# Gated linear attention and a token/channel mixer on one core: decays by small DMAs, the last batch's transposes by DMA, and a fixed instruction list

## The chip, the cores and the metric

The kernel runs on one core of a Trainium2 chip. The metric is device time in microseconds (us) of one execution, the median of three runs. The engines are TensorE (PE), VectorE (DVE), ScalarE (ACT), GpSimd (POOL) and SyncE (SP); each works through its own instructions in order and waits on semaphores for the others. Here POOL issues the input loads, SP issues stores and some loads.

## The reference

Inputs q, k, v and f_logit have 4 batches, 8 heads, 768 tokens and 48 features per head. Then follows a mixer over tokens and channels with four weight matrices.

```python
f = 1.0 / (1.0 + np.exp(-f_logit))
for t in range(S):
    state = f[:, :, t, :, None] * state + np.einsum('bhd,bhe->bhde', k[:, :, t], v[:, :, t])
    y[:, :, t] = np.einsum('bhd,bhde->bhe', q[:, :, t], state)
...
h = np.maximum(xt @ w_tok1, 0.0) @ w_tok2          # over tokens
u = x + h.transpose(0, 2, 1)
h2 = np.maximum(u @ w_ch1, 0.0) @ w_ch2            # over channels, 384 -> 1536 -> 384
out = u + h2
```

Here x is y with its 8 heads laid side by side, 768 x 384 per batch.

## The kernel before, in words

The 768 tokens of a batch b are cut into 6 chunks c of 128. Line numbers are those of the kernel before.

- *Gates* (L448): ACT makes L = ln(1 + exp(-f_logit)) with two passes (L455, L456). L is kept in fp32; its upper 16 bits are read as a bf16 number, and DVE or POOL puts the remainder into Llo (L461). Batch 0's chunks 3 to 5 use the fp32 form instead.
- *Sums* (L514): a matmul with a triangular matrix gives the running sum over the chunk's tokens (L528 and L529, or L517 in fp32). Beside it, for all chunks but the last, single-column matmuls with a vector of ones give the total over the chunk for each feature (L526, L527, or L519 in fp32), already laid out with features on partitions.
- ACT makes G = exp(-sum), Gi = exp(sum) (L539, L541) and from the totals glast = exp(-total), the decay of the state over the chunk (L544, 128 x 4).
- DVE makes q x G and k x Gi (L549). PE transposes both with an identity matrix, 8 transposes of 128 x 128 per chunk (L559); DVE or ACT copies the result from PSUM to qkT (L566, L572).
- *Scores* (L478): 8 matmuls of qkT with itself; DVE multiplies them by the triangle into AmT (L596). *Parts* (L494): k^T v for the state.
- *State* (L605, L608, L610 on DVE): state = (state + part) x glast. Two copies spread it into a block-diagonal bf16 tile (L615).
- *y* (L627, L634): qkT times the spread state, plus AmT times v; copied to x_bf and x_nat.
- *Mixer* per batch (L659): tok1 (L664), relu to h1T, tok2 (L680), sums into x_nat and u_bf, transposes of u_bf (L715) into uT, then ch1 (L732, 72 matmuls of 384 columns), relu to zT (L444 on ACT, L446 on DVE), ch2 (L751, 75 matmuls), the sum on DVE (L757) and the store by SP (L761).

The order of all work comes from a planner in the kernel (`Plan`, L104): each operation has a rank, costs per engine and a set of operations before it, and a table SHIFTS replaces rank and lag of some. The planner repeatedly takes the operation and engine with the earliest start plus lag, then the lowest rank, and emits the operations in the order of their planned starts. Where it sees PE idle in the first 25.5 us, it fills in dummy matmuls (L798). Work of neighbouring batches is interleaved: the attention of batch b + 1 runs between the ch1 and ch2 matmuls of batch b.

Loads: SP loads f of batch 0 chunk by chunk, held back by marks that POOL sets (L363); POOL loads k, q, v of batch 0 by chunk, the weights, and the later batches, those of batch 3 whole (L377, L384). The DMA on POOL's queue also casts fp32 to bf16. The triangle and the identity are made on POOL by a library (masks.py).

Of the kernel before, what the change touches and what calls it, by code (L numbers as in the profile page):

```python
# [16 lines left out]
WAKE = {PE: 55, ACT: 38, DVE: 38, POOL: 66, SP: 30}  # L17
NBANK = 8
RING = 16384
SHIFTS = (  # L20
# [57 lines left out]
)  # L78
KEPT = 3
SPLIT = 3  # L80


class Op:
    def __init__(self, engines, rank, fn, need, make, bank, kind):
        self.engines, self.rank, self.fn, self.kind = engines, rank, fn, kind
        self.need, self.make, self.bank = need, make, bank
        self.before: set = set()
        self.behind = None
        self.after: list = []
        self.missing = 0  # L90
        self.start = self.end = None
        self.engine = None
        self.tail = None
        self.room = 1
        self.lag = 0.0


class Bank:
    def __init__(self):
        self.users = 0  # L100
        self.at = None


class Plan:  # L104

    def __init__(self):  # L110
        self.ops = []
        self.maker: dict = {}
        self.users: dict = {}
        self.loads = {POOL: [], SP: []}

    def add(self, engines, rank, fn, need=(), make=(), bank=None, kind=("fix", 100, 100), tail_of=None, room=1):


        engines = (engines,) if isinstance(engines, str) else engines
        op = Op(engines, rank, fn, need, make, bank, kind)  # L120
        for key in need:
# [710 lines left out]
```

## Time and profile before

| | |
|---|---|
| Median of 3 runs | 182.77 us (182.35 to 183.07) |
| Span of the profiled execution, first to last instruction | 180.3 us |
| What lies around the span, from the median | 2.5 us |
| PE busy, matmuls | 171.1 us, 1811 |
| DVE, ACT, POOL busy | 129.6, 109.4, 86.2 us |
| First ch1 matmul (L732) starts | 34.20 us |
| Packets of POOL's DMA queue, share of 16 engines' span | 97.7% |

The record gives no other time of the profiled execution than its span, so the 2.5 us is the median less that span. Busy time of PE is the union of its matmuls' durations, and these overlap: a 384-column matmul is listed with 326 ns. The chain that ended last follows the work back from the last instruction; its rows give start, length and what it was. A releaser behind an arrow is what ended a wait.

### The profile page before, as it was taken

The page shows a single profiled execution, that of the slowest core. Times are in us where ns is not written, and L with a number is a line of the kernel's source. Part 1 is how long each engine was busy: PE and PEld are TensorE (multiplying, and loading weights), DVE is VectorE, ACT ScalarE, POOL GpSimd, SP SyncE. Part 2 cuts the span into 40 slices and gives each one's busy share as a digit, 9 for nine tenths or more (in the row PEclk, how much of TensorE's full clock was granted, in tenths as well). Part 3 has the DMA queues.
Part 4 walks back from the last instruction along what each step waited for, and adds up shares of the span by engine and source line. Part 5 has one row for each costly group of instructions (what it writes and reads, how often), then busy time and mean ns, then how long its engine had stood idle before and what let it go on. Part 6 is the DMA issues. An engine that isn't in the chain of part 4 may idle for free.

```text
span 180.3 us, 4528 instructions
## 1 busy us (share of the span) xinstructions
PE 171.1 (95%) x1811; PEld 111.4 (62%) x1811; DVE 129.6 (72%) x284; ACT 109.4 (61%) x266; POOL 86.2 (48%) x113
## 2 busy tenths in 40 slices
PE   6789998899999999999979999999999999999992
PEld 2356765556676667566746666766676656665661
DVE  6679886958898889997977837997677256652222
ACT  4677983689974698968399366356771233546000
POOL 7999699248399569879177501422030111100000
PEclk9999999999999999999999999999999999999999
DMA  7999999999999999969999921111000200400123
GB/s 103 133 173 157 146 202 230 219 147 197 157 138 187 240 192 87 148 76 138 194 109 126 133 77 44 47 44 47 0 0 5 87 0 4 175 0 0 47 88 131
DMA packets 88820, 19.95 MB, mean 111 GB/s; under 512 B 81536, under 2 KB 87984, under 8 KB 88800
## 3 DMA queue, kind: packets, MB, share of 16 engines
q0 software_dynamic: 78960, 13.77, 97.7%
q1 hardware_dynamic: 9840, 5.90, 11.0%
q8 instruction: 14, 0.23, 0.6%
q14 instruction: 6, 0.05, 0.1%
HBM read 25.17 MB, written 4.72 MB: 166 GB/s over the span
## 4 chain that ended last, share of the span: by engine, by line
PE 79%; DVE 6%; ACT 4%; issue 3%; POOL 3%; DMA 2%; DVEq 0%; POOLq 0%; ACTq 0%
PE ps L732 25%; PE ps L751 24%; PE ps L559 5%; PE ps L680 4%; PE ps L664 4%; PE ps L478 3%; DMA qk_sb<-in_q_dram 2%; DVE AmT L596 2%; PE ps L715 2%; PE ps L634 2%; PE ps L528 2%; PE ps L529 2%; PE ps L494 2%; POOL qk_sb L377 1%; PE ps L517 1%
## 5 line engine op out<-in xcount | busy, mean ns | idle before, releaser
L751 PE MATMUL ps<-w_ch,zT 128*128 128x384 bf16 (+2 forms) x300 | 53.0, 319 | 1.0 <-ACT zT L444 1.0
L732 PE MATMUL ps<-uT,w_ch 128*128 128x384 bf16 x288 | 51.6, 326 | 0.1
L444 ACT ACTIVATE zT<-ps 128x384 bf16<-128x384 f32 x70 | 33.6, 491 | 18.6 <-PE ps L732 13.9
L751 PEld LDWEIGHTS <-zT 128*128 128x128 bf16 x300 | 27.8, 98 | 17.5 <-issue 1.4
L732 PEld LDWEIGHTS <-w_ch 128*128 128x128 bf16 x288 | 27.0, 98 | 17.1 <-issue 0.5
L596 DVE TENSOR_TENSOR AmT<-ps,tri_bf 128x512 bf16<-128x512 f32 x46 | 29.7, 684 | 5.6 <-PE ps L478 3.5
L377 POOL DMA_DIRECT2D qk_sb<-in_q_dram x19 | 18.5, 974 | 10.9 <-issue 4.4
L757 DVE TENSOR_TENSOR x_nat<-x_nat,ps 128x384 f32<-128x384 f32 (+2 forms) x25 | 13.2, 534 | 11.7 <-PE ps L751 11.7
L377 POOL DMA_DIRECT2D qk_sb<-in_k_dram x19 | 18.8, 988 | 5.5 <-DMA f_sb<-in_f_logit_dram 4.5
L377 POOL DMA_DIRECT2D v_sb<-in_v_dram x19 | 18.7, 984 | 0.9 <-issue 0.9
L439 POOL CAST state_bd<-state 48x192 bf16<-48x192 f32 x17 | 6.4, 377 | 26.6 <-DVE state L610 22.3
L446 DVE TENSOR_SCALAR zT<-ps 128x384 bf16<-128x384 f32 x26 | 13.8, 554 | 5.7 <-PE ps L732 5.4
L549 DVE TENSOR_TENSOR qk<-qk_sb,GG 128x768 bf16<-128x768 bf16 (+1 forms) x30 | 13.9, 471 | 4.7 <-ACT GG L541 4.0
L559 PE MATMUL ps<-ident,qk 128*128 128x128 bf16 x192 | 14.7, 219 | 0.9 <-DVE qk L549 0.9
L539 ACT ACTIVATE GG<-ps 128x384 bf16<-128x384 f32 x24 | 11.7, 489 | 5.7 <-PE ps L529 3.9
L455 ACT ACTIVATE f_sb<-f_sb 128x384 f32<-128x384 f32 x24 | 11.8, 519 | 4.8 <-DMA f_sb<-in_f_logit_dram 4.7
L559 PEld LDWEIGHTS <-qk 128*128 128x128 bf16 x192 | 12.0, 98 | 4.3 <-DVE qk L549 2.2
L572 DVE COPY qkT<-ps 128x1024 bf16<-128x1024 bf16 x18 | 12.3, 685 | 1.9 <-PE ps L627 1.1
L541 ACT ACTIVATE GG<-ps 128x384 bf16<-128x384 f32 x24 | 11.7, 492 | 2.0 <-issue 1.8
L439 POOL CAST u_bf<-x_nat 128x384 bf16<-128x384 f32 x6 | 3.3, 550 | 20.0 <-DVE x_nat L696 20.0
L696 DVE TENSOR_TENSOR x_nat<-x_nat,ps 128x384 f32<-128x384 f32 x21 | 10.7, 549 | 2.9 <-PE ps L680 2.9
L456 ACT ACTIVATE L<-f_sb 128x384 f32<-128x384 f32 x24 | 12.1, 520 | 0.2
(71 smaller groups left out, 261.8 us busy)
## 6 DMA issues: line engine op xcount, KB each, us to landing
out_dram<-x_nat SPq DMA_DIRECT2D x23, 192.0 KB, 1.8
f_sb<-in_f_logit_dram POOLq DMA_DIRECT2D x3, 1152.0 KB, 11.1
qk_sb<-in_k_dram POOLq DMA_DIRECT2D x18, 96.0 KB, 6.4
qk_sb<-in_q_dram POOLq DMA_DIRECT2D x18, 96.0 KB, 6.1
v_sb<-in_v_dram POOLq DMA_DIRECT2D x18, 96.0 KB, 5.9
f_sb<-in_f_logit_dram SPq DMA_DIRECT2D x6, 192.0 KB, 4.2
w_ch<-in_moe_w_ch_dram POOLq DMA_DIRECT2D x2, 576.0 KB, 9.7
w_ch<-in_moe_w_ch_dram POOLq DMA_DIRECT2D x1, 1152.0 KB, 14.9
```

Of the source, the lines that this page charges most:

```text
L377: lambda eng=eng, into=into, of=of: eng.dma_start(out=into, in_=of),
L444: nc.scalar.activation(out_, in_, AF.Relu, bias=0.0, scale=1.0)
L446: nc.vector.tensor_scalar(out_, in_, 0.0, None, ALU.max)
L455: add(ACT, r, lambda: nc.scalar.activation(fb, fb, AF.Exp, bias=0.0, scale=-1.0), make=[key], kind=el)
L456: add(ACT, r, lambda: nc.scalar.activation(full, fb, AF.Ln, bias=1.0, scale=1.0), need=[key], make=[whole], kind=el)
L549: add(DVE, r, lambda n=n: nc.vector.tensor_tensor(qk[i][:, n, :, 0:D], qk_sb[nb][:, n, :, c, :], GG[i][:, n], ALU.mult), need=[(x, nb, c) ...
L559: nc.tensor.transpose(to[:, o + hp, :], blk(src)[:, hp, :], ident)
L572: add(DVE, r, lambda: nc.vector.tensor_copy(qkT[i], banks[p_t[0].at].bitcast(BF16).rearrange("p (n t) -> p n t", t=C)), make=[("qkT", i, 0 ...
L596: add(DVE, r, lambda half=half, made=made: nc.vector.tensor_tensor(half, made(), tb4, ALU.mult), need=["tri_bf"], make=[("AmT", i, p)], ba ...
L732: nc.tensor.matmul(banks[pm.at][:, 0:384], lhsT=w[:, kt, c0:c0 + 128], rhs=uT[:, kt, cols], start=(kt == 0), stop=(kt == 2))
L751: nc.tensor.matmul(banks[pm.at][:, 0:n1 - n0], lhsT=zT[:, kt, tt * 128:(tt + 1) * 128], rhs=w_ch2[:, kt, n0:n1], start=(kt == 0), stop=(kt ...
L757: add(DVE, rank("ch2", tt), lambda un=un, pm=pm, n=n1 - n0: nc.vector.tensor_tensor(un, un, banks[pm.at][:, 0:n], ALU.add), make=[("x_nat" ...
```

## The change

Four things change. The names of operations in the changed kernel are tuples such as ("state", b, c).

1. *Totals.* They are kept for batch 0's chunks 0 to 2 alone (TOTALS). Elsewhere the last row of the running sum is the total: ACT takes the exponential of partitions 96 to 127 of the sum (32 x 384, reordered) into a tile grow, and SP sends row 127 of it to glast, 128 partitions x 4 numbers.
2. *Transposes of batch 3.* Instead of 8 PE transposes and a copy per chunk, one transposing DMA from SP turns all 1024 columns of qk into qkT.
3. *Order.* The planner is gone. ORDER is a fixed list of all operations: a number is the operation in the order in which they are added, a letter chooses the engine (A ACT, D DVE, G POOL), a number after a colon the PSUM bank, and z12 stands for 12 dummy matmuls. Which engine does which copy changes with it, as do the orders of chunks, loads and stores. Dummy matmuls are 35, all ahead of batch 0's mixer. More operations may run on either of ACT and DVE, and spreads on DVE too.
4. *Start and buffers.* SP issues batch 0's six f loads without marks. The triangle is made by a DVE memset and one POOL instruction, the first on POOL ahead of its loads; the identity comes from the triangle by DVE. Llo has 10 buffers of one chunk. The loads of w_tok1 and w_tok2 move ahead of v of chunk 5.

```diff
+    grow = [st([128, 2, 64, HP], FP32, f"grow{i}") for i in range(NROW)]
...
-            if not last:
+            if (b, c) in TOTALS:
                 bh, bl = blk(hi_c), blk(lo_c)
                 for hp in range(HP):
                     g = pm[:, DM + hp:DM + hp + 1]
                     nc.tensor.matmul(g, lhsT=bh[:, hp, :], rhs=ones_bf, start=True, stop=False)
                     nc.tensor.matmul(g, lhsT=bl[:, hp, :], rhs=ones_bf, start=False, stop=True)
...
+        if not last and (b, c) not in TOTALS:
+            r = (b * (NCH - 1) + c) % NROW
+            add(("grow", b, c), ACT, lambda: nc.scalar.activation(
+                grow[r][96:128, :, 0:D, :],
+                banks[p_s.at][96:128, 0:DM].rearrange("t (hp par d) -> t par d hp", par=2, d=D), AF.Exp, bias=0.0, scale=-1.0),
+                make=[("grow", r)], bank=p_s, kind=el)
+            add(("glast", b, c), SP, lambda: nc.sync.dma_start(
+                out=glast[g4], in_=grow[r][127:128].rearrange("o par x hp -> o (par x) hp")),
+                need=[("grow", r)], make=[("glast", g4)], kind=("fix", 430, 3900))
...
+        if b in TURNED:
+            add(("turn", b, c), SP, lambda: nc.sync.dma_start_transpose(
+                out=qkT[it], in_=qk[i].rearrange("t n h d -> t (n h d)")), need=[("qh", i), ("kh", i)],
+                make=[("qkT", it, 0), ("qkT", it, 1)], kind=("fix", 430, 4500))
+            return [Bank(), Bank()]
...
-    for op in plan.best(idle, 6500.0, 25500.0):
-        op.fn()
+    plan.run(idle)
...
+        for token in ORDER.split():
+            if token[0] == "z":
+                idle(int(token[1:]))
+                continue
+            token, *at = token.split(":")
...
+            op = self.ops[int(token)]
...
+            op.fn()
...
+22 25 18 24 17 23 26 13 14 15 27 0 7 1 20 29 51 5 11 2 3 10 8 28 60 52 30 61 53D 57 6 9 z12 104:0 31 16 54 55 35 166:1
```

By engine, the changed kernel has 24 totals (152 before), 144 transposes for qkT (192), 35 dummy matmuls (31), 50 relus of zT on DVE (26), 17 small DMAs and 6 transposing DMAs on SP. On SP their order is: six f loads, decays 0.3, 0.4 (batch.chunk), 1.0 to 1.4, then decays of batch 2 and stores of batch 0 in turn, decays 3.1 and 3.0, turn 3.0, a store, turn 3.1, decay 3.2, turn 3.2, a store, turn 3.3, a store, decays 3.3 and 3.4, a store, turn 3.5, a store, turn 3.4, and the other stores.

More of the change, by code (lines that the diff above doesn't have):

```diff
@@ L83, with __init__ @@
+"""
 class Op:
-    def __init__(self, engines, rank, fn, need, make, bank, kind):
-        self.engines, self.rank, self.fn, self.kind = engines, rank, fn, kind
-        self.need, self.make, self.bank = need, make, bank
+    def __init__(self, name, engines, fn, bank, kind):
+        self.name, self.engines, self.fn, self.bank, self.kind = name, engines, fn, bank, kind
+        self.second = None
         self.before: set = set()
[L88 to L95, printed above, removed]
+        self.engine = engines[0]
@@ L98 @@
 class Bank:
[L99 to L101 removed]
+    at = None
 class Plan:
@@ L113, in __init__, with add @@
         self.users: dict = {}
-        self.loads = {POOL: [], SP: []}
-    def add(self, engines, rank, fn, need=(), make=(), bank=None, kind=("fix", 100, 100), tail_of=None, room=1):
+    def add(self, name, engines, fn, need=(), make=(), bank=None, kind=("fix", 100, 100)):
         engines = (engines,) if isinstance(engines, str) else engines
-        op = Op(engines, rank, fn, need, make, bank, kind)
+        op = Op(name, engines, fn, bank, kind)
         for key in need:
@@ L132, in add @@
         if bank is not None:
-            key = bank
-            if key in self.maker:
-                op.before.add(self.maker[key])
+            if bank in self.maker:
+                op.before.add(self.maker[bank])
             if engines == (PE,):
-                self.maker[key] = op
-        if kind[0] == "load":
-            line = self.loads[engines[0]]
-            if line:
-                op.behind = line[-1]
-            line.append(op)
-        op.room = room
-        if tail_of is not None:
-            while tail_of is not None:
-                tail_of.before |= op.before - {tail_of}
-                tail_of.tail = tail_of.tail or op
-                tail_of = next((x for x in self.ops if x.tail is tail_of), None)
+                self.maker[bank] = op
@@ new lines, in run @@
+    def run(self, idle):
+        letters = {e[0]: e for e in (ACT, DVE)} | {"G": POOL}
+        for token in ORDER.split():
[3 more added lines that the diff above has]
+            token, *at = token.split(":")
+            if token[-1].isalpha():
+                token, engine = token[:-1], letters[token[-1]]
+            else:
+                engine = None
+            op = self.ops[int(token)]
+            op.engine = engine or op.engines[0]
+            for bank, number in zip([x for x in (op.bank, op.second) if x is not None and x.at is None], at):
+                bank.at = int(number)
+            op.fn()
@@ L394 @@
-    mark(2)
-    load("f", 0, 2, SP)
-    load("v", 0, 0)
-    add(POOL, -6.0, lambda: make_upper_triangular(nc, tri, val=1.0, diag=True), make=["tri"],
-        kind=("load", 720, 720, 0))
-    once(DVE, lambda: nc.vector.tensor_copy(tri_bf, tri), ["tri_bf"], 200)
-    plan.ops[-1].before.add(plan.ops[-2])
-    add(POOL, -6.0, lambda: make_identity(nc, ident), make=["ident"], kind=("load", 870, 870, 0))
-    for c in range(1, NCH):
-        load("kq", 0, c)
-        if c + 2 < NCH:
-            mark(c + 2)
-            load("f", 0, c + 2, SP)
-        load("v", 0, c)
@@ L408, with once, memset @@
-    loaded = add(POOL, 9.0, lambda: None, kind=("load", 1, 0, 0))
-    nc.vector.memset(steady, 1.0)
-    once(DVE, lambda: nc.vector.memset(ones_bf, 1.0), ["ones_bf"], 60)
-    once(DVE, lambda: nc.vector.memset(ones, 1.0), ["ones"], 60)
+            make=[name], kind=("load", 900, 1024, size))
+    def once(name, engine, fn, make, own, need=()):
+        return add(("once", name), engine, fn, make=make, need=need, kind=("fix", own, own))
+    def memset(name, tl, value, make, own):
+        once(name, DVE, lambda: nc.vector.memset(tl, value), make, own)
@@ new lines @@
+    nc.vector.memset(steady, 1.0)
+    base = tri if SPLIT < NCH else tri_bf
+    memset("tri", base, 0.0, ["tri"], 180)
+    once("tri", POOL, lambda: nc.gpsimd.affine_select(out=base, in_=base, compare_op=ALU.is_gt, fill=1.0, base=0,
+                                                      pattern=[[-1, C]], channel_multiplier=1), ["tri"], 310)
+    if SPLIT < NCH:
+        once("tri_bf", DVE, lambda: nc.vector.tensor_copy(tri_bf, tri), ["tri_bf"], 200, ["tri"])
+    else:
+        plan.maker["tri_bf"] = plan.maker["tri"]
@@ new lines @@
+    once("ident", DVE, lambda: nc.vector.tensor_tensor(ident[:, 1:C], tri_bf[:, 1:C], tri_bf[:, 0:C - 1], ALU.subtract),
+         ["ident"], 200, ["tri_bf"])
+    once("ident0", DVE, lambda: nc.vector.tensor_copy(ident[:, 0:1], tri_bf[:, 0:1]), ["ident"], 70, ["tri_bf"])
+    memset("ones_bf", ones_bf, 1.0, ["ones_bf"], 60)
+    if SPLIT < NCH:
+        memset("ones", ones, 1.0, ["ones"], 60)
+    for b, c in sorted(TOTALS):
+        memset(f"L{b}{c}", L[b % 2][:, c, :, D:64], 0.0, [("L", b % 2, c)], 200)
@@ new lines @@
+    for i in sorted({place(b, c) for b, c in TOTALS if b or c < SPLIT}):
+        memset(f"Llo{i}", Llo[i][:, :, D:64], 0.0, [("Llo", i)], 120)
+    for i in range(NROW):
+        memset(f"grow{i}", grow[i][96:128], 1.0, [("grow", i)], 600)
+    for i in range(len(state_bd)):
+        memset(f"sbd{i}", state_bd[i], 0.0, [("sbd", i)], 220)
+    for c in range(FSP):
+        if c >= MARK:
+            add(("mark", c), POOL, lambda c=c: nc.gpsimd.memset(f_sb[0][0:1, 0:1, c, 0:1], 0.0), make=[("f", 0, c)],
+                kind=("fix", 90, 90))
+        load("f", 0, c, SP)
@@ L419 @@
+    for cs in LOADS0F:
+        load("f", 0, cs)
+    if HOLD is not None:
+        add(("hold",), POOL, lambda: nc.gpsimd.tensor_copy(held, f_sb[0][0:1, 0, HOLD, 0:1]), need=[("f", 0, HOLD)],
+            make=["held"], kind=("fix", 100, 100))
+    for cs in LOADS0K:
+        load("kqv", 0, cs)
     load_w("w_tok1", w_tok1, moe_w_tok1, 1900)
@@ L446, in relu, with copies, gates @@
             nc.vector.tensor_scalar(out_, in_, 0.0, None, ALU.max)
-    def gates(b, c, r):
+    def copies(name, engines, out_, in_, need=(), make=(), bank=None, kind=None, fn=copy_on):
+        op = add(name, engines, None, need=need, make=make, bank=bank, kind=kind)
+        op.fn = lambda: fn(op.engine, out_(), in_())
+    def gates(b, c):
         fb = f_sb[b % 2][:, :, c, :]
@@ L481, in attention @@
         for k, c in enumerate(cs):
-            own = 212 if k else 330
-            chain = add(PE, due(b, cs[0]), lambda c=c, k=k: scores(c % 2, heads[k]), need=need, bank=heads[k][1],
-                        kind=("mm", own if live else own + 107, own), tail_of=chain)
-            plan.maker[heads[k][0]] = chain
+            op = add(("scores", b, c), PE, lambda c=c, k=k: scores(at(b, c), heads[k]),
+                     need=[("qkT", at(b, c), p) for p in range(2)], bank=heads[k][1], kind=("mm", 223, 223, 1))
+            plan.maker[heads[k][0]] = op
+            op.second = heads[k][0]
         def dg(k):
@@ L529, in sums @@
             nc.tensor.matmul(pm[:, 0:DM], lhsT=tri_bf, rhs=lo_c[:, :, 0:D], start=False, stop=True)
-        add(PE, r, sums, need=[lk, "tri_bf", "ones_bf", rk] if split else ["tri", "ones", lk], bank=p_s, room=3,
-            kind=mms(*([1] * (0 if last else 8 if split else 16)), *[DM] * (2 if split else 4)))
-        plan.ops[-1].before.update(chains[-2:-1])
+        add(("sums", b, c), PE, sums, need=[lk, "tri_bf", "ones_bf", rk] if split else ["tri", "ones", lk], bank=p_s,
+            kind=mms(*([1] * (8 if (b, c) in TOTALS else 0)), *[DM] * 2) if split else ("mm", 750 + (950 if (b, c) in TOTALS else 0)))
         def sview():
@@ L615, in rest @@
-                op.fn = lambda op=op, rows=rows, cols=cols: copy_on(
-                    op.engine, state_bd[i][rows, :, cols], state[rows])
-        p_y = Bank()
-        def y():
-            return banks[p_y.at][:, 0:DM]
-        def before():
-            yh = y().rearrange("t (h e) -> t h e", e=D)
-            for hp in range(HP):
-                nc.tensor.matmul(yh[:, 2 * hp:2 * hp + 2, :], lhsT=qkT[i][:, hp, :],
-                                 rhs=state_bd[(c - 1) % 2][:, hp, :],
+                copies(("spread", b, c, cols.start), (ACT, POOL, DVE), lambda rows=rows, cols=cols: state_bd[j][rows, :, cols],
+                       lambda rows=rows: state[rows], need=["state", ("sbd", j)], make=[("sbd", j, cols.start)],
+                       kind=("el", HP * D, False, 1.01))
@@ L629, in before, with y_into @@
+        def y_into(bank, before=True):
+            yh = banks[bank.at][:, 0:DM].rearrange("t (h e) -> t h e", e=D)
+            for hp in range(HP if c else 0):
+                nc.tensor.matmul(yh[:, 2 * hp:2 * hp + 2, :], lhsT=qkT[it][:, hp, :],
+                                 rhs=state_bd[bd(b, c - 1)][:, hp, :],
                                  start=(hp == 0), stop=False, skip_group_check=True)
-        def within():
-            yh = y().rearrange("t (h e) -> t h e", e=D)
             for h in range(H):
-                nc.tensor.matmul(yh[:, h, :], lhsT=AmT[i][:, (h % 2) * 4 + h // 2, :],
+                nc.tensor.matmul(yh[:, h, :], lhsT=AmT[it][:, (h % 2) * 4 + h // 2, :],
@@ L782 @@
+                    need=[("x_nat", xn, tt)] if end else [], bank=pm, kind=("el", n1 - n0, True, 1))
+                add(("store", b, tt, n0), SP, lambda un=un, to=to: nc.sync.dma_start(out=to, in_=un),
+                    need=[("x_nat", xn, tt, n0) if end else ("x_nat", xn, tt)], kind=("store", 350, 2000, 480))
     for b in range(B):
         for c in range(NCH):
-            gates(b, c, due(b, c) - 3.0)
-        if b == 0:
-            load("f", 2)
-            for c in range(NCH):
-                load("kqv", 2, c)
@@ L789 @@
-        if b == 1:
-            load("fkqv", 3)
+            gates(b, c)
+        for what, nxt, cs in LOADS[b]:
+            load(what, nxt, cs)
         step = 2 if b else 1
         for c in range(0, NCH, step):
-            attention(b, range(c, c + step), due)
-        mixer(b, ranks(b))
+            attention(b, range(c, c + step))
+        mixer(b)
     def idle(n):
```

449 lines of the change are left out of this document (175 added, 274 removed), and 57 rows, old and new, of the table SHIFTS.

## The prediction

> **What bounds the kernel now.** I read the page first, its busy times, then the chain of work that ended last.
>
> ```profile
> PE 171.1 (95%) x1811; PEld 111.4 (62%) x1811; DVE 129.6 (72%) x284; ACT 109.4 (61%) x266; POOL 86.2 (48%) x113
> ...
> PE 79%; DVE 6%; ACT 4%; issue 3%; POOL 3%; DMA 2%; DVEq 0%; POOLq 0%; ACTq 0%
> ```
>
> TensorE is 95% busy and 79% of the chain. A busy PE is not PE at its peak, so I took the steps at which matmuls really follow each other from dense stretches of the chain, listed in order of time:
>
> ```profile
> 13.93 0.80 PE ps L519 x8
> ...
> 34.20 1.64 PE ps L732 x9
> ...
> 47.34 0.55 PE ps L478 x16
> 47.90 0.36 PE ps L494 x16
> ...
> 113.10 0.89 PE ps L559 x16
> ...
> 157.97 7.31 PE ps L732 x45
> 165.28 10.91 PE ps L751 x72
> ```
>
> A matmul of 384 columns costs 7.31/45 = 0.162 us, a transpose 0.89/16 = 0.056, a score 0.034, a state part 0.0225. The single-column totals come from the timeline of PE (start, duration):
>
> ```profile
> 11.39 0.17 PE L526 MATMUL ps<-ones_bf,L 128*128 128x1 bf16 x1
> ...
> 11.59 0.33 PE L528 MATMUL ps<-L,tri_bf 128*128 128x384 bf16 x1
> ```
>
> Eight totals start within 11.39 to 11.59: 0.025 each, although their rows show 165 ns of duration. In the same way a y matmul costs 0.042 (state side) or 0.025 (AmT side).
>
> Now the work from 34.20, the first ch1, to 176.20, where PE leaves the chain: 142.0 us. 672 matmuls of 384 columns 109.1; 24 narrower ones of the last tile 2.0; 198 transposes 11.0; 144 scores 5.0; 120 parts 2.7; 120 totals 3.0; y 60 x 0.042 + 144 x 0.025 = 6.1. Sum 138.9. **So PE idles 3.1 us in 142**: there the kernel is bound by the number of PE instructions, and what is removed there is saved, if nothing new makes PE wait. Before 34.20 it is a chain over all engines, with 31 filling matmuls (L798). After 176.20 come two sums and a store, 4.1 us. 34.2 + 138.9 + 3.1 + 4.1 = 180.3, the span. The median of the runs, 182.77, is 2.5 us above it; I add 2.5 at the end.
>
> **Part 1, totals.** 120 single-column bf16 matmuls go from batches 1 to 3: 120 x 0.025 = 3.0 us, all inside the PE-bound stretch. The 8 fp32 ones of batch 0, chunks 3 and 4, were 0.80 + 0.79 us on the chain in front of 34.20. In exchange ACT makes 17 exponentials of 32 x 384. No row has 32 partitions in that permuted order; between 0.18 us (glast, L544) and 0.49 (a full G, L539) I take the second, with a step of 0.37 instead of 0.05: 17 x 0.32 = 5.4 us more ACT.
>
> Then 17 DMAs of 128 x 16 bytes go through SP, each with a landing that the state update on DVE waits for. Nearest rows, the 192 KB stores, first in a stretch with full DMA queues (52 to 66 us), then after 100 us:
>
> ```profile
> out_dram<-x_nat SPq DMA_DIRECT2D x4, 192.0 KB, 5.1
> ```
>
> ```profile
> out_dram<-x_nat SPq DMA_DIRECT2D x17, 192.0 KB, 1.8
> ```
>
> So 1.6 (the 48 KB store) to 7.6 us (the longest store under load); I take 4, nearer to the loaded median because before 100 us the queues are full. How far ahead are they? I counted the PE work that stands in the fixed list between each transfer and its state update: 3.8 us for batch 1 chunk 0, 4.7 for chunk 2, 5.0 for batch 2 chunk 0, 5.6 to 17 for the rest (batch 0, chunk 3: 12). At 4 us one is 0.2 late: nothing.
> [...] The store rows (5.1 against 1.8) show a price of load, but cannot show what a packet of 16 bytes pays. [...]
>
> **Part 2, transposes of batch 3.** 48 x 0.056 = 2.7 us of PE and 6 DVE copies (0.68 each, L572) go, in the PE-bound stretch. Six transposing DMAs of 256 KB come, on SP, between stores. Behind each on SP stand a store or a small transfer; behind its landing, the scores. The list leaves between transfer and scores 4.5, 4.9 and 4.8 us of PE work in the tighter one of each pair. No row shows a transposing transfer. From below: 256/192 of an unloaded store, 2.4 us. From above: the POOL loads under backlog, 12.5 us. I take 4.5, near the SP loads of f (192 KB in 192-byte pieces, median 4.2): just hidden.
> [...]
>
> **Part 3, the new list.** ACT gives 24 relus of zT to DVE, takes 5 of the 1024-wide copies, 11 of uT; DVE takes 13 spreads of the state. Counting by steps of back-to-back rows (mask 0.60, 384 columns 0.465 on DVE, 0.37 or 0.41 on ACT), the 50 us after 44.2 hold 46.9 us of DVE (42.1 in the trace) and 43.1 of ACT (34.1). The busy times by window (length, PE, PEld, DVE, ACT, POOL, clock, DMA share, GB/s) show the fullest ten of those 50 us in the trace, and a later stretch with room:
>
> ```profile
> 64.20:74.20 10.00, 10.00 (x136) 6.82 (x135) 9.16 (x20) 9.20 (x25) 9.36 (x12) 1.00 1.77 144
> ...
> 114.20:134.20 20.00, 20.00 (x242) 13.76 (x241) 16.48 (x36) 12.74 (x29) 3.57 (x9) 1.00 0.09 31
> ```
>
> So 46.9 in 50 has to run a little denser than DVE ever did here (9.16 in 10) while PE stays full. I take it as fitting; a rival has the other case.
> The start: SP issues six f loads at once; POOL's first load now stands behind the triangle, which waits for seven DVE memsets. By the memset rows (0.66 us for 768 columns) that is about 3.4 us instead of 1.33, but the f loads fill the wire meanwhile; the two token-mixer weights go ahead of the last v. First sums 1.5 us later, fp32 totals 1.6 shorter, tok1 half done early. I take 0, between -2 and +2. The fills (35 against 31) stand in this front only, where PE waits anyhow.
>
> **Sum**: 180.3 - 3.0 - 2.7 = 174.6 of span, idle time as before; with 2.5 around it **177.1 us**. Idle and front move it by about 3.5 either way.
>
> **Rivals.**
> - *Transposing transfers late.* For: unseen kind, 256 KB. Against: the DMA share is 0.09 after 114 us. With a landing of L, PE loses 3L - 14.2. It decides from L = 6.9 (then 183.7, slower); at 8 us 186.9.
> - *Small decays late.* DVE is in order: behind the waiting state update stand the masks that y needs. At 7.6 us, the loaded maximum, the excesses are 3.8 + 2.9 + 2.6, and 2.0 for batch 2 chunk 4: 11.3, of which, as an estimate, PE's other work covers a third: 184.6. It turns slower at about 6.6 us net, a landing near 7.2.
> - *DVE the bound.* At the trace's fullest rate, 9.16 in 10, 46.9 take 51.2 us, at the mean rate of that stretch (42.1 in 50) 55.7: 1.2 to 5.7 more, the middle 3.5, 181. For: both helpers are full at once there. Against: PE idles only 3.1 us now with DVE at 84%.
> - *More than that.* The list also packs away the idle 3.1 (1.1 of it one wait at 91.4 for zT) and shortens the front by 1 to 2: 173.
> - *The change does not do it.* The order of instructions shows 24 totals and 144 transposes left, so this is out.
>
> **How the numbers follow.** Forecast 0.60 (173.5 to 180.5), transposes late 0.10, decays late 0.08, DVE bound 0.12, more 0.10. About 0.5% either way (181.9 to 183.7) is what measurement can tell from no change. Faster: 0.60 + 0.10 + two thirds of DVE bound = 0.78. Same: the rest of that, 0.04. Slower: 0.18. The range, 172.8 to 184.5, leaves out the late transposes, half of the late decays and a tail below.
>
> **What would show it.** Right: L405/L406 with only 24 totals beside them, PE steps unchanged, PE idle after the first ch1 near 3 us, glast landing under 5 us, scores of batch 3 not waiting for DMA. Wrong: a wait of state or mask on DMA glast, of scores on DMA qkT, DVE over 96% between 44 and 94 us, or a first ch1 after 36 us.

## The result, and the profile after

The changed kernel took 190.47 us (median of five runs, 189.52 to 193.51), the kernel before 182.94 us on the same chip: ratio 1.0377, 95% interval 1.033 to 1.0423. By that ratio it is 6.9 us slower, where 177.1 us and a gain were predicted. The profiled execution of the changed kernel is a slow one (193.51 us, span 191.7; the three that were compared have spans of 187.5 to 188.4), so its profile is 3 to 4 us longer than theirs, and what is read in it is checked below against the profiles of its variants.

The page after, busy times and the chain that ended last:

```profile
PE 171.5 (89%) x1627; PEld 106.2 (55%) x1631; DVE 136.6 (71%) x297; ACT 112.3 (59%) x257; POOL 85.1 (44%) x104
...
PE 44%; DMA 10%; DVE 4%; ACT 3%; POOL 2%; issue 1%; SPq 1%; DVEq 0%
```

The shares are of the span, and the chain after can be followed back only to 62.46 us. From there on TensorE has 109 of the chain's 115 us before and 85 of 124 after; transfers have none before and 18.5 us after. The windows (length, PE, PEld, DVE, ACT, POOL, clock, DMA share, GB/s) show where:

```profile
64.20:74.20 10.00, 10.00 (x105) 6.44 (x103) 9.19 (x19) 8.73 (x22) 6.94 (x7) 1.00 2.24 117
84.20:94.20 10.00, 8.40 (x85) 5.72 (x85) 8.20 (x14) 7.68 (x17) 9.73 (x9) 0.83 1.05 74
114.20:134.20 20.00, 17.72 (x179) 10.73 (x178) 13.52 (x30) 10.47 (x25) 2.94 (x5) 0.91 0.46 91
```

In the first stretch PE is as busy as before. In the other two it is not full, and its granted clock is under 1. What PE waited for (us in total, times, longest):

```profile
PE ps L609 <- ACT zT L324: 2.4, 1, 2.4
PE ps L357 <- DVE qkT L318: 2.4, 2, 2.2
PE ps L373 <- DMA v_sb<-in_v_dram: 1.9, 1, 1.9
...
PE ps L357 <- DVE zT L326: 1.5, 1, 1.5
...
PE ps L373 <- DVE zT L326: 0.9, 2, 0.5
...
PE ps L357 <- DMA qkT<-qk: 0.4, 1, 0.4
```

After the first ch1, the only long wait before was 1.0 us for zT. I split each profile as in the prediction: first ch1; PE's work after it, a count of matmuls times the prediction's steps; gaps between starts beyond the step, over 0.17 us (waits), 0.12 to 0.17 us (mostly matmuls at half clock: from 85.46 us those of 384 columns follow each other in 0.320 us, where the step is 0.162) or less; and the time from the last matmul's end to the end of the span. The parts add up to the span within 0.4 us:

| kernel | first ch1 | work | waits | half clock | small | after PE | span | ratio to before |
|---|---|---|---|---|---|---|---|---|
| before | 34.2 | 138.6 | 1.8 | 0.1 | 2.2 | 3.2 | 180.3 | 1 |
| changed | 33.9 | 132.9 | 11.9 | 4.5 | 2.4 | 5.8 | 191.7 | 1.0377 |
| e1 spreads on ACT | 35.9 | 132.9 | 8.8 | 2.9 | 2.4 | 4.8 | 187.8 | 1.0217 [1.0128, 1.0306] |
| e2 totals | 35.1 | 135.9 | 5.9 | 0.1 | 1.7 | 3.9 | 182.8 | 1.0031 [0.9994, 1.0069] |
| e3 transposes on PE | 34.3 | 135.6 | 8.2 | 0.5 | 2.2 | 3.9 | 184.8 | 1.0171 [1.009, 1.0253] |
| e4 both back | 33.5 | 138.6 | 3.8 | 0.3 | 2.1 | 4.3 | 182.7 | 1.008 [1.004, 1.012] |
| e5 awake (6.5 of dummies) | 33.9 | 132.9 | 5.7 | 0.5 | 2.5 | 4.9 | 187.0 | 1.0383 [1.0336, 1.043] |
| e6 totals in batch 2 | 34.5 | 133.9 | 8.5 | 0.2 | 1.8 | 4.8 | 183.8 | 1.0152 [1.011, 1.0194] |
| e9 load of v early | 33.9 | 132.9 | 7.6 | 1.4 | 2.7 | 6.3 | 184.9 | 1.0221 [1.0153, 1.0289] |
| e14 e1 and e9 | 35.5 | 132.9 | 6.0 | 1.7 | 2.8 | 4.8 | 183.8 | 1.0111 [1.0075, 1.0147] |
| e17 e14, waits moved | 35.1 | 132.9 | 6.4 | 0.5 | 2.1 | 5.9 | 183.0 | 1.0058 [1.0025, 1.0092] |
| e16 | 33.9 | 135.9 | 3.8 | 0.3 | 2.0 | 3.3 | 179.4 | 0.9906 [0.9877, 0.9936] |
| e18 | 34.3 | 133.9 | 3.5 | 0.5 | 2.5 | 4.1 | 178.9 | 0.9867 [0.9841, 0.9892] |

So the work did go: 5.7 us less than before, as predicted (3.0 and 2.7), and in dense rows the steps are the old ones (four matmuls of 384 columns in 0.65 us at 101.50). In the profiled execution it was given back as waits (10.1 more), half clock (4.4) and a longer end (2.6).

The first ch1 now waits for a load. The second load of w_ch lands at 33.89 in the changed kernel, and ch1 starts at 33.94; before, it landed at 32.63, 1.6 us ahead of ch1. In e1, e14, e17 and e13 the landing comes later (34.6 to 35.8), and ch1 with it.

Four places in the changed kernel's trace made the theories. *A, GpSimd holds up VectorE.* Timelines of DVE and of POOL (start, duration):

```profile
53.27 1.46 DVE L499 TENSOR_TENSOR state<-tsum,glast 128x192 f32<-128x192 f32 x1
54.77 2.01 DVE L318 CAST state_bd<-state 48x192 bf16<-48x192 f32 x1
```

```profile
53.66 0.85 POOL L346 TENSOR_TENSOR Llo<-L 128x384 bf16<-128x384 f32 x1
54.45 2.27 POOL L251 DMA_DIRECT2D f_sb<-in_f_logit_dram  x1
```

The state update takes 0.35 elsewhere, the spread 0.26. The spread ends with the issue of the load beside it. PE waits 2.7 us at 55 to 58 for the copy behind them, and 2.3 at 92 to 94, behind two more such instructions (1.34 at 88.42, 1.55 at 90.24). The spread at 54 to 56 is as long in other runs: 2.03 us in e3, 2.01 in e5, 1.54 in e6 and e9. *B, late decays*, from the timelines of DVE and ACT:

```profile
82.82 0.36 DVE L494 TENSOR_TENSOR state<-ps,glast 128x192 f32<-128x192 f32 x1 [2.04 <-DMA glast<-grow]
```

```profile
82.72 0.48 ACT L421 ACTIVATE grow<-ps 32x384 f32<-32x384 f32 x1 [2.34 <-DMA glast<-grow]
```

The first two transfers of batch 2, issued at 75.43 and 75.95, landed at 82.53 and 82.69. A load of f was in flight from 71.61; it landed at 82.36, just ahead of them. The issues in two windows at 71.6 and 75.4 (size, us to landing):

```profile
f_sb<-in_f_logit_dram POOLq DMA_DIRECT2D x1, 1152.0 KB, 10.8
...
glast<-grow SPq DMA_DIRECT2D x1, 2.0 KB, 7.1
```

In all eight profiles that have this transfer beside this load (the changed kernel, e1, e3, e5, e9, e13, e14, e17) it lands 0.15 to 0.21 us after the load. VectorE waits for the value, ScalarE for a row buffer (there are three) that the same landing frees, and the relus of zT stand behind both. *C and F, transfers beside each other*: the timelines of SP and POOL.

```profile
109.86 1.43 SPq L447 DMA_TRANSPOSE qkT<-qk  x1
...
112.18 2.32 SPq L447 DMA_TRANSPOSE qkT<-qk  x1
```

```profile
106.50 2.25 POOL L251 DMA_DIRECT2D v_sb<-in_v_dram  x1
```

C is that the transposing transfers cost by themselves, F that they and the load of v hold each other up. These two transposing transfers took 6.5 and 6.1 us from issue to landing, the other four 3.05 to 3.08. The load of v of batch 3, which the list puts behind spreads on POOL, took 10.9 and landed at 117.41. *E, the clock*: 0.50 for some 3.4 us after the idle stretches at 81, 92 and 115 us (from 84.65, 94.89 and 118.78, 3.41 us each). (D is that the list itself is too tight.)

### The profile page after: what moved, and what is told of

Read it like the earlier page. It is cut to its first block, busy times and chain, and to the rows that moved or that the text cites. A ratio compares the mean times of both kernels' runs of the same rounds, so it can differ in the third digit from the quotient of the medians.

```text
span 191.7 us, 4198 instructions
## 1 busy us (share of the span) xinstructions
PE 171.5 (89%) x1627; PEld 106.2 (55%) x1631; DVE 136.6 (71%) x297; ACT 112.3 (59%) x257; POOL 85.1 (44%) x104
## 4 chain that ended last, share of the span: by engine, by line
PE 44%; DMA 10%; DVE 4%; ACT 3%; POOL 2%; issue 1%; SPq 1%; DVEq 0%
PE ps L627 17%; PE ps L609 16%; DMA glast<-grow 4%; DMA qkT<-qk 3%; DMA v_sb<-in_v_dram 2%; PE ps L561 2%; PE ps L545 2%; PE ps L593 1%; PE ps L357 1%; PE ps L513 1%; PE ps L444 1%; DMA out_dram<-x_nat 1%; DVE zT L326 1%; POOL qk_sb L251 1%; DVE state_bd L318 1%
## 5 line engine op out<-in xcount | busy, mean ns | idle before, releaser
L609 PE MATMUL ps<-uT,w_ch 128*128 128x384 bf16 x288 | 55.1, 337 | 2.4 <-ACT zT L324 2.4
L627 PE MATMUL ps<-w_ch,zT 128*128 128x384 bf16 (+2 forms) x300 | 55.4, 325 | 0.1
L324 ACT ACTIVATE zT<-ps 128x384 bf16<-128x384 f32 x46 | 21.6, 492 | 20.3 <-PE ps L609 20.1
L326 DVE TENSOR_SCALAR zT<-ps 128x384 bf16<-128x384 f32 x50 | 25.6, 550 | 9.4 <-PE ps L609 9.3
L251 POOL DMA_DIRECT2D qk_sb<-in_k_dram x19 | 18.5, 977 | 4.6 <-DMA f_sb<-in_f_logit_dram 4.6
L320 POOL CAST u_bf<-x_nat 128x384 bf16<-128x384 f32 x11 | 6.1, 559 | 26.2 <-DVE x_nat L577 26.2
L320 POOL CAST state_bd<-state 48x192 bf16<-48x192 f32 x10 | 3.4, 343 | 30.3 <-PE ps L373 17.9
L417 ACT ACTIVATE GG<-ps 128x384 bf16<-128x384 f32 x24 | 11.9, 499 | 5.0 <-PE ps L406 4.9
L545 PE MATMUL ps<-x_bf,w_tok 128*128 128x384 bf16 x48 | 13.3, 325 | 0.5 <-DVE AmT L485 0.3
L338 ACT ACTIVATE f_sb<-f_sb 128x384 f32<-128x384 f32 x24 | 11.9, 520 | 2.9 <-DMA f_sb<-in_f_logit_dram 2.9
L357 PE MATMUL ps<-qkT 48*128 48x128 bf16 x192 | 8.5, 218 | 4.8 <-DVE qkT L318 2.4
L444 PE MATMUL ps<-ident,qk 128*128 128x128 bf16 x144 | 11.8, 224 | 1.0 <-DVE qk L434 0.9
L346 POOL TENSOR_TENSOR Llo<-L 128x384 bf16<-128x384 f32 x11 | 9.5, 870 | 6.4 <-ACT L L339 6.2
```

Of the source, the lines that this page charges most:

```text
L251: lambda eng=eng, into=into, of=of: eng.dma_start(out=into, in_=of),
L324: nc.scalar.activation(out_, in_, AF.Relu, bias=0.0, scale=1.0)
L326: nc.vector.tensor_scalar(out_, in_, 0.0, None, ALU.max)
L338: add(("exp", b, c), ACT, lambda: nc.scalar.activation(fb, fb, AF.Exp, bias=0.0, scale=-1.0), make=[key], kind=el)
L417: add(("Gi", b, c), ACT, lambda: nc.scalar.activation(Gi[i], sview(), AF.Exp, bias=0.0, scale=1.0), make=[("Gi", i)], bank=p_s, kind=el)
L444: nc.tensor.transpose(to[:, o + hp, :], blk(src)[:, hp, :], ident)
```

## The experiments

Lines in the quoted rows are each kernel's own.

**e1: spreads.** In the list, the 13 spreads marked D become A:

```diff
-... 120D ... 140D ... 141D ... 398D ... 408D ... 652D ... 651D ... 953D ...
+... 120A ... 140A ... 141A ... 398A ... 408A ... 652A ... 651A ... 953A ...
```

> The changed kernel, with the 13 spreads that its list gives to DVE given to ACT at the same places (ACT makes 13 x 0.3 = 4 us more). Theory A, that DVE is held up by GpSimd beside it: four of DVE's instructions took 1.3 to 2.0 us instead of 0.26 to 0.35 there, and PE waited for their consequences at 55.0, 57.7, 91.8 and 93.9 us, 5.0 us in all, and ran two stretches at half rate behind it, 1.6 us each: 183 to 186 us, no DVE instruction on state over 0.6 us. Theory B, the small decays that land late, and theory C, the transposing transfers: 190 to 191, or up to 192 with ACT fuller. Theory D, the list is too tight for its helpers whatever they are: 190 to 192, with ACT waits in place of DVE's.

187.91 us, ratio 1.0217 against 1.0377. The waits at 55 and 92 us are gone; one of 0.9 us for ACT came at 57. The gain is less than A expected (183 to 186). The profile holds 2.0 us of delay ahead of the first ch1, where w_ch lands at 35.82; whether the three moved spreads of batch 0 did that, or chance, isn't shown. The waits of B and F stay as they were (wait rows of e1):

```profile
PE ps L610 <- ACT zT L325: 2.3, 1, 2.3
PE ps L374 <- DMA v_sb<-in_v_dram: 1.9, 1, 1.9
```

**e2, e3, e4: the parts undone.** e2: `TOTALS` again for batches 1 to 3 (single-column matmuls in `sums`, ACT's 4 exponentials, no transfer; DVE also clears the padding that totals read). e3: 8 PE transposes and a copy per chunk of batch 3. e4: both.

```diff
-            if (b, c) in TOTALS:
+            if (b, c) in TOTALS or (b, c) in TOTALS2:
...
-            add(("turn", b, c), SP, lambda: nc.sync.dma_start_transpose(
+            plan.extra.setdefault(first, []).append(flip)
```

> The changed kernel, with the decays of batches 1 to 3 by totals on PE and 4 exponentials on ACT as before (120 matmuls of one column, 3.0 us; 15 transfers and 15 exponentials of 32 x 384 less). Theory B, small decays land late: the wait of 2.6 us at 81.4 and the 1.6 us at half rate behind it go, as do waits of DVE and ACT for landings, 5 to 7 us off and 3.0 on: 186.5 to 188.5. Theory A (GpSimd holds up DVE): 3.0 on, 2 to 4 off: 189.5 to 191.5, the waits at 55 and 92 stay. Theories C and D: about 193.5.

> The changed kernel, with batch 3's 48 transposes on PE again (2.7 us) and 6 copies on DVE and ACT (0.7 to 1 us each). Theory C, the transposing transfers and what stands behind them on SP: waits of 0.6, 0.6 and 0.3 us at 117.7 and 144 go and with them the stores that held x_nat, 2.7 on: 191 to 192; if they cost much more than the waits show, under 190. Theories A, B and D: 193.

> The changed kernel with both parts undone, so that the list, the engines chosen in it and the start remain. By all theories PE has 5.7 us more work than in the changed kernel. Theory D (the list): 194 to 196. Theory A: 191 to 194. Theories B or C as the only cause: 183 to 186, as fast as the kernel before.

183.98, 186.66 and 185.54 us. With both back the list costs 0.8%, not 6%, so D falls: the list alone is nearly as good as the planner. On it, the transposing transfers gain (e4 to e2, 1.008 to 1.0031) and the small decays lose (e4 to e3, to 1.0171); in the medians that is 1.6 and 1.1 us, and the intervals of the ratios overlap. Both together lose far more (1.0377) than the sum of the two, 1.012. One reading, not shown by a run of its own: each part takes PE work away and so makes the same helpers' results due sooner. e2 came out better than any theory had it. e3 lies in the second branch of C (under 190): in the full change the transfers cost more than the waits for them.

**e5: the clock.** `y5x5` is five dummies into bank 5:

```diff
-673:4 535A 672:5 685 655A 674:2 852 ...
+673:4 535A y5x5 672:5 685 655A y2x2 674:2 852 ...
```

> The changed kernel, with 34 more dummy matmuls of 512 columns into free banks, in front of the instructions at which PE waited at 55, 58, 81, 92, 94, 115 and 118 us (up to 9 in one place, 0.216 us each, fewer than the waits are long). They compute nothing that is used. Theory E, half the damage is TensorE's clock: after idle stretches of 2.3 us and more it was granted at 0.50 for about 3.4 us, which costs 1.6 to 1.7 us each, two to three times in a run. With the dummies the waits stay but the clock holds at 1.00: 185.5 to 187.5. If the half rate has another reason, or if the waits shift and the dummies stand in the way: 190 to 193.

189.82 us, ratio 1.0383: no gain, though the windows show the clock at 1.00:

```profile
84.00:94.00 10.00, 9.84 (x114) 6.12 (x114) 8.04 (x16) 6.91 (x16) 9.17 (x9) 1.00 0.91 67
114.00:124.00 10.00, 9.35 (x104) 5.82 (x103) 7.37 (x17) 4.80 (x12) 2.44 (x4) 1.00 0.34 62
```

So E gets no support: awake, PE was no faster. But the run isn't clean. At 81 us the dummies themselves waited 1.5 us for a bank that ACT had yet to read, ran from 83.17, and PE took up ch1 at 85.11, while the first zT it needed was made at 83.50. These 1.6 us are as much as one stretch at half clock costs by the expectation. At 57 to 58 and 115 to 116 us PE went on within 0.2 us of what it waited for. What half clock costs by itself stays open.

**e6: decays of batch 2 alone by totals.**

```diff
+TOTALS2 = [(2, c) for c in range(5)]
```

> The changed kernel, with the decays of batch 2 alone by totals on PE (40 matmuls of one column, 1.0 us); those of batches 1 and 3 stay small transfers. Theory B1, what costs is the late landing of batch 2 (7.1 and 6.7 us beside the 1.1 MB load of f): the wait of 2.6 us at 81 and the half rate behind it go: 186 to 187.5, most of what all totals gave (184.0). Theory B2, what costs is the added work on ACT and the order on SP in all batches: a third of it, 188 to 189.5.

185.98 us, ratio 1.0152 against 1.0377, with 1.0 us of PE work more. B1 holds: the wait of 2.6 us at 81 is gone, and its half clock too; what is left waits behind spreads (55 to 58, and 88 to 91 behind one of 1.67 us) and for v and qkT (110 to 113).

**e7, e12, e15: the transposing transfer in the kernel before.** e7 and e12 put it at the place of the PE transposes, e7 with 4.5 us told to the planner; e15 at the place of the copy:

```diff
-            add(DVE, r, lambda: nc.vector.tensor_copy(
+            add(DVE, r, lambda: nc.sync.dma_start_transpose(
+                out=qkT[i], in_=qk[i].rearrange("t n h d -> t (n h d)")) if b == 3 else nc.vector.tensor_copy(
```

> The kernel before with its planner, and batch 3's transposes by one transposing transfer per chunk from SP; the planner is told 4.5 us for it and orders the rest anew. PE has 2.7 us less. If the transfers are hidden, as in the changed kernel with totals, where they gave 1.5 of 2.7: 180.5 to 182. If the rank table, made for the other order, fits badly: 183 to 187.

> The kernel before in exactly its old order, with batch 3's transposes by transposing transfers from SP at the places of the old ones; PE has 2.7 us less, but its order leaves only what stood between transposes and scores to hide 3.05 us of transfer. If PE waits for each pair of chunks as long as the transfer is longer than the old path of 8 transposes and a copy (about 1.2 us), 1.5 to 2 us three times: 184 to 186. If other PE work covers it: 180.5 to 182.

> The kernel before, every instruction in the old order; batch 3's 8 transposes per chunk are gone and a transposing transfer on SP stands where the copy to qkT stood, so it is sent a little later than the copy began. Unloaded it lands after 3.05 us, where transposes and copy took about 1.5: if nothing covers it, PE waits 1 to 2 us for each of the 6 chunks and saves 2.7: 184 to 190. If other PE work in between covers it: 180.5 to 182.

199.54, 197.05 and 186.58 us. In e7 and e12 the planner moved the last chunks of batch 3 behind the mixer work that should cover them (their scores run at 143 to 154 us instead of 128 to 137, presumably because qkT's buffer is needed earlier), and PE waited 14 to 15 us, of it 0.8 for qkT in e12: these two tell of the order, not of the transfer, and e12 was not "exactly the old order" as its expectation says. e15 keeps the order, and what PE waits for anew is the transfers alone (wait rows of e15):

```profile
PE ps L478 <- DMA qkT<-qk: 3.7, 4, 1.3
```

The waits are 5.0 us more than before in the table's sense (6.8 against 1.8), with 2.7 less work: without other work in front of the scores the transfer loses. The list of the changed kernel has that work.

**e8: small decays in the kernel before**, at the places of the old exponentials:

```diff
+                nc.scalar.activation(gr[96:128, :, 0:D, :], ...
+                nc.sync.dma_start(out=glast[g4], in_=gr[127:128].rearrange("o par x hp -> o (par x) hp"))
```

> The kernel before with its planner and order, and the decays of batches 1 to 3 by small transfers at the places of the old exponentials (two row buffers). PE has 3.0 us less, ACT 15 x 0.44 = 6.6 more, and each state update waits for a landing of 2 to 7 us that the order doesn't know of. Theory B (late landings): slower, 186 to 192, with waits of the state updates for the transfers in all three batches. If landings are hidden: 180 to 182.

190.40 us, ratio 1.044 [1.0396, 1.0484]. The time is as B said, the place is not: no state update waits long, ACT waits for its two row buffers (wait rows of e8), and what stands behind it is late:

```profile
ACT grow L551 <- DMA glast<-grow: 5.1, 3, 2.0
```

**e9, e14: the load of v, and with it the spreads.** One token moves (e14: e1's change too):

```diff
-... 851G ... 688G ... 714G ... 715G ... 375 ...
+... 851G 375 ... 688G ... 714G ... 715G ...
```

> The changed kernel, with one instruction moved: GpSimd issues the load of v of batch 3 right after the second remainder of batch 3, some 7 us earlier, ahead of the spreads it stood behind. Theory F, the load and the first transposing transfers hold each other up: the load took 10.9 us from issue to landing, the two transfers beside it 6.5 and 6.1 us against 3.05 for the other four, and PE waited 2.6 us for both at 115 to 118: these waits go, the transfers take 3 to 4 us: 187 to 189. If DVE and ACT are late there anyhow, as at 55 to 95 us: 190.

> The changed kernel with both parts of the change, but the 13 spreads on ACT (e1) and the load of v issued earlier (e9). If the losses add: 190.3 - 2.6 - 2.9 = 185. What is then left over the kernel before (183) belongs to the small decays (wait for glast at 81 us) and the list. If the helpers are the bound and the waits only move: 187.

187.17 and 185.20 us. In e9 the transposing transfers land after 3.23 and 3.06 us (6.5 and 6.3 in e1, with v as late as ever) and the wait at 115 to 118 is gone: F holds. e14 shows that A and F add up nearly (0.016 of the ratio each alone, 0.027 together). Left are the wait for w_ch ahead of the first ch1 (1.5 us), the end, and the wait behind the late decay, as long as ever (wait rows of e14):

```profile
PE ps L610 <- ACT zT L325: 2.3, 1, 2.3
```

**e11, e13: ACT's time or the landing.** e11 adds the row exponentials to e2 and leaves their result unread; e13 lets ACT's 4 exponentials go through a small transfer:

```diff
+                gsmall[r], banks[p_s.at][:, DM:DM + HP], AF.Exp, bias=0.0, scale=-1.0))
+            add(("glast", b, c), SP, lambda: nc.sync.dma_start(out=glast[g4], in_=gsmall[r]))
```

> The changed kernel with decays by totals (184.0), and ACT also makes the 15 exponentials of 32 x 384, whose result nothing reads; no small transfer is sent for batches 1 to 3. ACT has 15 x 0.49 = 7.4 us more than with totals alone. Theory B, the landing is what costs: 184 to 185. Theory G, ACT's added time is what costs: 187 to 190.

> The changed kernel with totals on PE for batches 1 to 3 and ACT's 4 exponentials of them, as in the run with totals (184.0); but ACT writes them into a side buffer, and a small transfer from SP (128 partitions x 16 bytes, as in the change) brings them to where the state update reads them. ACT has nothing more to do, and each update waits for a landing. Theory B, the landings cost what ACT's time (2.7 us) leaves of the 9.5: 187 to 190. If only both together cost: 184 to 185.5.

186.70 and 184.26 us. A transfer by itself costs nothing that can be seen: e13 (1.0036) is as fast as e2. It doesn't show that a late landing is free, for here it wasn't late. The load of f landed at 80.55 instead of 82.36, the first transfer of batch 2 at 80.74, after 6.3 us, and DVE came to it at 81.05; ACT waits 0.2 us for its buffer:

```profile
80.95 0.17 ACT L435 ACTIVATE gsmall<-ps 128x4 f32<-128x4 f32 x1 [0.21 <-DMA glast<-gsmall]
```

ACT's added time in e11 costs 2.7 us, but not plainly as ACT time: its longest PE wait (2.3 us at 87) stands behind a state update that took 2.02 us beside a POOL remainder and a spread of 1.54, which the shift had brought together. How much of the 2.7 is ACT alone stays open.

**e17: what waits, moved.** e14, with these tokens later:

```diff
-541D 667 526:7 666 641 668 539A 649 530:6 643G ... 531D 670:1 639 525A ... 529A 701:6
+541D 526:7 666 539A 530:6 ... 531D 670:1 639 641 649 643G 525A ... 529A 667 668 701:6
```

> As e14 (both parts of the change, spreads on ACT, the load of v early: 185.2), with five instructions of batch 2 later in the list: the first state update and the next sum on VectorE with one spread on GpSimd behind three later relus and masks, and the fourth row exponential on ACT with its transfer behind three relus of zT. The landing itself stays near 7 us. Theory H, what costs is not the landing but what stands behind those who wait for it: the wait of 2.5 us at 81 goes or falls under 0.8: 182.5 to 183.5. If the wait only moves to the next instruction: 185.

184.77 us, 1.0058 against 1.0111. The first landing still takes 6.9 us, but the 2.3 us for zT is gone from the wait rows: H holds for that wait. The time missed what H expected (182.5 to 183.5), and the two intervals overlap. In sum the waits did not fall (6.4 against 6.0), for one of 1.4 us for a mask came at 102; half clock fell from 1.7 to 0.5, PE ended at 177.1 instead of 179.0, and the end after PE grew from 4.8 to 5.9.

**e10, e16, e18: what the findings point to.** e10: e2, v early, four spreads on ACT. e16: three spreads (408, 651, 652), and three ready stores earlier on SP. e18: as e16, but totals in batch 2 alone.

```diff
-... 348 ... 343 ... 601 ... 840 ... 596 ... 835 ...
+... 348 343 ... 601 596 ... 840 835 ...
```

> The changed kernel with all three suspects out: decays of batches 1 to 3 by totals, the load of v of batch 3 issued earlier as in the run before, and the four spreads on DVE at 52 to 93 us on ACT. The transposing transfers and the list stay. With totals alone it took 184.0, and PE still waited 1.8 us at 89 (behind slow spreads), 1.7 at 111 (v and qkT), 1.4 at 69, 0.9 at 137. If theories A (GpSimd holds up DVE) and F (load against transfers) hold: 180 to 181.5, faster than the kernel before. If the waits only move on: 183 to 184.5.

> As e10 (totals for batches 1 to 3, the load of v early), but only the three spreads that were held up go to ACT (the fourth, on ACT, made PE wait 1.8 us at 68), and three stores that had long been ready move forward on SP: two stood among the last nine, whose issue takes 0.5 us each and ends the kernel, one held up x_nat at 134 us. 1.0 off at the end, 0.6 at 134, 0.5 to 1.5 at 68: 181 to 182.5. If the waits only move on: 183 to 184.

> As e16 (181.4), but only batch 2 has its decays by totals; those of batches 1 and 3 are small transfers as in the change. PE has 2.0 us less, ACT 10 x 0.31 = 3.1 more. If landings outside the loaded stretch are free: 179.5 to 181. If ACT's added time in batch 1 counts as it did in e11 (2.7 for three batches): 181.5 to 183.

183.69 us for e10 (1.0012 [0.9979, 1.0045]), short of what was expected: the waits moved on, 1.8 us to a spread now late on ACT (69) and 1.6 to a mask (102). 181.43 us for e16 (0.9906) and **180.86 us for e18 (0.9867 [0.9841, 0.9892]), faster than both kernels**. With the stores out of the last queue, e16 ends 3.3 us after PE. e18's page:

```profile
PE 168.7 (94%) x1671; PEld 105.5 (59%) x1671; DVE 133.2 (74%) x310; ACT 111.4 (62%) x260; POOL 85.0 (48%) x104
```

## Why the prediction was wrong

- **Right: the steps, the counts and, by luck, the front.** The work fell by 5.7 us as predicted. First ch1 came at 33.9 (34.2 predicted), but not along the chain that I had reasoned with: it waits for the second load of w_ch, which I had not looked at.
- **The step that failed is "idle time as before" in the sum.** In the place of 3.1 us of idle after the first ch1 (here 1.8 of waits and 2.3 in small pieces) the changed kernel has 18.8 in its profiled execution (11.9, 4.5 and 2.4), and its variants e1, e3 and e9 have 10.9 to 14.1. Two of the signs I had named for being wrong came: a wait of the state update on DMA glast (2.04 us) and one of scores on DMA qkT (0.4). The three rivals were priced as exclusive cases with 0.08 to 0.12 each; in fact late decays, late transposes and a delayed DVE came together between 55 and 118 us, and the two parts of the change cost more together than apart (e2, e3, e4).
- **"At 4 us one is 0.2 late: nothing."** The first two landings of batch 2 took 7.1 and 6.7 us, inside the bounds I gave (1.6 to 7.6). The cover was counted well: 7.1 less the 5.0 us I had for batch 2 chunk 0 is 2.1, and VectorE waited 2.04. The term that was mis-sized is the landing: I went by a median, and these landings follow the load in flight. The trace before had it: the store of 7.6 us, issued at 56.35, landed at 64.00, 0.3 us after a load of f (issued at 52.63, landed at 63.69). The issues before, in the windows 52 to 66 and at 56.3:

```profile
f_sb<-in_f_logit_dram POOLq DMA_DIRECT2D x1, 1152.0 KB, 11.1
...
out_dram<-x_nat SPq DMA_DIRECT2D x1, 192.0 KB, 7.6
```

And I counted cover for the state update alone; the trace shows a second waiter, ACT at its row buffers, and in e17 the wait of PE goes when less stands behind the two. Undoing batch 2 alone takes 0.022 off the ratio (e6).
- **"46.9 of DVE's 50 us ... taken as fitting."** The rival feared that DVE would be too full; what came is that its instructions were held up. I had no row of a spread on DVE, and four of DVE's instructions on state took 5.1 us more than elsewhere. The sign I had named, DVE over 96% between 44 and 94 us, did not come: 44.1 of the 50 us, against 44.6 before. Only ten of the 50 were that full (54 to 64), and that is no sign of harm by itself, for the kernel before has ten as full with PE at 10.00. So "denser than DVE ever did here (9.16 in 10)" was a wrong reading, from windows that began every ten us. The windows, after and then before:

```profile
54.00:64.00 10.00, 7.61 (x99) 4.96 (x97) 9.88 (x17) 4.65 (x12) 8.83 (x9) 1.00 1.32 160
```

```profile
73.10:83.10 10.00, 10.00 (x106) 6.42 (x105) 9.81 (x24) 7.93 (x21) 7.84 (x9) 1.00 1.42 93
```

Taking the 13 spreads off DVE is worth 0.016 (e1).
- **"Just hidden" for the transposing transfers.** 3.05 us unloaded beats the 4.5 that I took. The argument against the rival, a DMA share of 0.09 after 114 us, was read from the order before; the new order had v of batch 3 in flight until 117.4. Worth 0.016 (e9).
- **The end.** I kept 4.1 us from 176.20. After PE's last matmul it took 3.2 us before, 5.8 in the changed kernel: nine stores were issued one behind the other from 183.29 on, two of them ready for long, and the last left at 188.74, 2.5 us after the last sum. Eight issues took 0.33 to 0.54 us, the second 1.51 (1.91 in e9); why, isn't shown. I had looked at SP's order for the transfers, not for the last stores. Moving the stores is part of e16 and e18; alone it wasn't tried.
- Not settled: how much of the 2.7 us in e11 is ACT's time, what half clock costs (e5), why the two parts cost more together than apart, and whether both parts in full with all cures beat e18.

## What to carry to other kernels

Taking work from the engine that is the bound can make all its helpers due sooner: price each helper's result against the new schedule, with every buffer it must win back, and not against the idle time of the old. A row's duration belongs to its engine and its neighbours (here a spread on VectorE took 0.26 us at 127.55, with no GpSimd work beside it, and 2.01 at 54.77, beside the issue of a load); an operation moved to an engine that never ran it here has no row yet. And a transfer's price is that of its hour (a small decay landed after 1.93 us at 129.03, with no load in flight, and after 7.10 at 75.43, beside one of 1152 KB): look at what the new order has in flight when it is issued, and when that lands, and not at a median of the old order.

## What the runs showed of the hardware

- Over all 20 profiles, a spread on VectorE (48 x 192, SBUF to SBUF) took 0.24 to 0.26 us in each of 40 cases with no GpSimd work beside most of it, up to 1.67 beside a remainder and up to 2.03 beside the issue of a load. Not every issue slows it: in the changed kernel the spreads at 19.39 and 52.04, each wholly beside one, took 0.26. The state update, two inputs in SBUF, had a median of 0.35 us beside load issues and of 0.69 (up to 2.02) beside remainders. Instructions with an input in PSUM were not held up in these profiles: sums (L497) never passed 0.36, masks 0.70, relus of zT 0.56. Why the other two are slowed isn't shown.
- In the changed kernel the waits of PE around 81 to 84, 92 to 95 and 115 to 118 us sum to 2.6, 2.3 and 2.6 us, and a granted clock of 0.50 followed for 3.41 us each, from 84.65, 94.89 and 118.78; waits of 2.7 in all at 55 to 58 were followed by none. The three starts lie 10.24 and 23.89 us apart, 3.0 and 7.0 times 3.41. e1, e9 and e14 show 3.41 us at 0.50 from 84.94, 83.82 and 85.86, after 2.2 to 2.5 us idle; e3 none after 2.2 us. What sets off the 0.50 isn't shown.
- A transfer of 128 x 16 bytes landed after 1.93 us at 129.03, with no load in flight, and after 7.10 at 75.43, beside a load of 1152 KB; in eight profiles it landed 0.15 to 0.21 us after that load. Not every transfer waits so: in the changed kernel three of the same size, issued at 54.01 to 55.23, landed at 57.22 to 57.57, ahead of the load of f whose issue began at 54.45 (64.30), and the store that the kernel before issues at 54.66 landed at 60.34, ahead of the load of f in flight (63.69). What decides it isn't shown.
